# Moving the weight tiles 96 bytes apart, and the probabilities by 32, in a kernel of attention and two feed-forward layers

## The chip, the cores and the metric

The kernel runs on one core of one Trainium2 chip. The metric is the device time of one launch in microseconds (us); lower is better. PE is TensorE, DVE is VectorE, ACT is ScalarE, POOL is GpSimd, SP is SyncE. SBUF is the on-chip memory; an address here is a byte offset inside a partition, the same in all 128 partitions.

## The reference

Three layers follow each other. `q`, `k` and `v` have 2 batches of 8 heads, 768 positions and width 64; `x` between the layers has 1536 tokens of width 512; the two hidden widths are 2048 and 1536.

```python
mask = q_bucket[:, :, :, None] == k_bucket[:, :, None, :]   # buckets: signs of q @ proj, k @ proj
scores = np.where(mask, scale * q @ k.T, -1e9)
attn = np.exp(scores - max); attn /= attn.sum(-1) + 1e-9
x = (attn @ v)                      # heads side by side: 1536 x 512
h = x @ w_in;  x = (h * np.cos(h)) @ w_out
g = x @ w_gate
out = (g * sigmoid(g) * (x @ w_val)) @ w_out2
```

All data are float32.

## The kernel before

The order of the work is written out by hand (the pools run in manual schedule), so each engine gets its instructions in the order in which the code issues them.

**Attention** (about 15 to 232 us of the trace). Two heads run as a pair. The scores of a block of 128 queries are four matmuls of 384 columns (lines 540 and 543), in a float32 form called float32r, with operands split into a high and a low part. DVE writes the block of probabilities `p` out of PSUM (L550), ACT applies the exponential in place (L561), POOL scales it in place (L579), PE transposes it in six pieces of 128 columns, plain float32 (L600, `t<-ident,p`: the identity `ident` is the moving operand, `p` the stationary one), and ACT or DVE copies the result. The product with `v` is L618.

**The first feed-forward layer** (about 232 to 483 us). For each of 48 pairs of token block and hidden block, `hidden` makes `h` and `out1` adds its product with `w_out`. The weights lie in tiles of two parts, high and low, of 128 x 512 each: ACT writes the high part, POOL the low one (`split_hi`). Each product is three matmuls, high by high, high by low, low by high (`each_of_three`, its matmul has line 804). In `h` and `out1` the weight tile is the stationary operand, 128 of its columns at a time, and the activations (`xh`, `xl`, `g..h`, `g..l`) move, 512 columns each. Twelve matmuls make one `h`, twelve the four pieces of one `out1`.

**The second feed-forward layer** (about 483 to 764 us). A form with seven products in place of eight makes `gate` and `val`: here too the weights (`prepare`, three tiles with tag `sp` and one with tag `sp4`) are stationary and activations of 384 columns move, six matmuls a product. Between them stand matmuls of `out2`, mostly in runs of six, where the activation `uh` or `ul` is stationary and the weight tile (tag `spo`, `prepare_out`) moves, 512 columns.

**Addresses.** A weight tile has 2 x 512 x 4 = 4096 bytes in each partition. The pool `late` holds three plain tiles `w`, six buffers `sp` from byte 130016 on, two buffers `raw`, and four buffers `spo` from 162784 on. In the built program every operand of every float32r matmul starts at a multiple of 512 bytes plus 480; the eight buffers of `p` start at a multiple of 512 plus 32 and `ident` at one plus 128.

Of the kernel before, what the change touches and what calls it, by code (L numbers as in the profile page):

```python
# [10 lines left out]
F32 = mybir.dt.float32  # L11
F32R = mybir.dt.float32r
# [5 lines left out]
P = 128  # L18
# [9 lines left out]
def lsh_attention_moe_moe2(  # L28
# [15 lines left out]
    NB = proj.shape[1]  # L44
    NT, DM = out.shape
# [18 lines left out]
    NL, NR = 3, 10  # L64
    NPP = NC2 // 2
    NSPO = 4

    ctx.enter_context(tc.manual_schedule())

# [32 lines left out]
    }  # L102
    done = {"fetch": 0}
    pools = {}

    def fetch_next():
        i = done["fetch"]
        if i == len(items):
            return
        done["fetch"] += 1  # L110
        nm, c = items[i]
        pool = pools["late"] if i >= NATT and i % 2 else early
        raw = pool.tile([P, DM, 2], I32, tag="raw", bufs=2, name=f"raw{i}")
        w = sources[nm].bitcast(I32)
        if nm in ("out", "out2"):
            nc.sync.dma_start(
                out=raw.rearrange("p f t -> p (f t)"), in_=w[c * P : (c + 1) * P, :]
            )
        else:
            nc.sync.dma_start(  # L120
                out=raw.rearrange("p (a f) t -> p a (f t)", a=NCC),
                in_=w.rearrange("(a p) f -> p a f", p=P)[:, :, 2 * c * P : 2 * (c + 1) * P],
            )
        raws[i] = raw
# [73 lines left out]
            fetched[nm, n] = t  # L198

    def split_hi(nm, n, pool=None, tag="sp", bufs=6):  # L200
        t = (pool or pools["late"]).tile([P, 2, DM], F32R, tag=tag, bufs=bufs, name=f"{nm}{n}s")
        w = fetched.pop((nm, n), None)
        if w is None:
            w = stored[nm, n % NC1]
        nc.scalar.activation(out=t[:, 0, :], in_=w, func=AF.Copy)
        parts[nm, n] = t
        return lambda: nc.gpsimd.tensor_tensor(
            out=t[:, 1, :], in0=w, in1=t[:, 0, :].bitcast(F32), op=ALU.subtract
        )

    def split(nm, n, **place):
        if (nm, n) not in parts:
            split_hi(nm, n, **place)()
# [10 lines left out]
    pre = actx.enter_context(tc.tile_pool(name="pre", bufs=1))  # L224
# [1 line left out]
    sm = actx.enter_context(tc.tile_pool(name="sm", bufs=4))  # L226

    pj0 = {nm: pre.tile([P, D], F32, tag="pj0" + nm, name="pj0" + nm) for nm in "qk"}
    pjs = pre.tile([P, NB], F32, tag="pjs", name="pjs")
    crow = pre.tile([1, 2, P], F32, tag="crow", name="crow")  # L230
    one = pre.tile([1, 1], F32, tag="one", name="one")

# [635 lines left out]
    for u in range(NU):  # L868
        pr, i = divmod(u, NBLK)
# [158 lines left out]
    def two_parts(t, src):  # L1028

        nc.scalar.activation(out=t[:, 0], in_=src, func=AF.Copy)  # L1030
        return lambda: nc.gpsimd.tensor_tensor(
            out=t[:, 1], in0=src, in1=t[:, 0].bitcast(F32), op=ALU.subtract
        )

    def prepare(nm, m):


        if m >= NSTEP:
            return
        p0, p1 = fetched.pop((nm, m, 0)), fetched.pop((nm, m, 1))  # L1040
        A11, A12, A21, A22 = p0[:, : 2 * P], p0[:, 2 * P :], p1[:, : 2 * P], p1[:, 2 * P :]
        x, y = (
            pools["right"].tile([P, 2, 2 * P], F32, tag="w", bufs=NR, name=f"{nm}{m}{a}")
            for a in "xy"
        )
        t = [
            pools["late"].tile([P, 2, 2, 2 * P], F32R, tag="sp", bufs=6, name=f"{nm}{m}t{i}")
            for i in range(3)
        ]
        t4 = pools["right"].tile([P, 2, 2 * P], F32R, tag="sp4", bufs=2, name=f"{nm}{m}t3")  # L1050

        pieces[nm, m] = {
            1: t[0][:, :, 0], 2: t[0][:, :, 1], 6: t[1][:, :, 0], 7: t[1][:, :, 1],
            5: t[2][:, :, 0], 3: t[2][:, :, 1], 4: t4,
        }
        lo = two_parts(t[0].rearrange("p t a f -> p t (a f)"), p0)
        nc.vector.tensor_tensor(out=y[:, 0], in0=A21, in1=A22, op=ALU.add)
        yield
        lo()
        (nc.gpsimd if (nm, m) == ("gate", 1) else nc.vector).tensor_tensor(out=x[:, 0], in0=y[:, 0], in1=A11, op=ALU.subtract)  # L1060
        yield
        nc.vector.tensor_tensor(out=x[:, 1], in0=A11, in1=A21, op=ALU.subtract)
        yield
        nc.vector.tensor_tensor(out=y[:, 1], in0=A12, in1=x[:, 0], op=ALU.subtract)
        lo = two_parts(t[1], x)
        yield
        lo()
        lo = two_parts(t[2], y)
        yield
        lo()  # L1070
        lo = two_parts(t4, A22)
        yield
        lo()

    def prepare_out(m, k):
        t = pools["late"].tile([P, 2, DM], F32R, tag="spo", bufs=NSPO, name=f"out2_{m}_{k}s")
        two_parts(t, fetched.pop(("out2", m, k)))()
        parts["out2", m, k] = t

# [114 lines left out]
    def out2(m, order=("11", "22", "21", "12")):  # L1194
# [9 lines left out]
        for i, q in enumerate(order):  # L1204
# [4 lines left out]
            for c in range(HB):  # L1209
                s, ts_ = half * HB + c, slice(c * P, (c + 1) * P)  # L1210
                ends = m == NSTEP - 1 and s == NBLK - 1
                if ends and seen:
                    for (pool, tag), cs in zip(banks, (slice(0, 2 * P), slice(2 * P, DM))):
# [4 lines left out]
                        o = pools["late"].tile(  # L1218
                            [P, 2 * P], F32, tag="spo", bufs=NSPO, name=f"ol{cs.start}"
                        )  # L1220
# [8 lines left out]
                if ends:  # L1229
                    part = pools["late"].tile([P, DM], F32, tag="spo", bufs=NSPO, name="olp")  # L1230
                    nc.scalar.activation(out=part, in_=acc[s], func=AF.Copy)
# [22 lines left out]
    for n in range(2, N1):  # L1254
# [10 lines left out]
        if n >= 3:  # L1265
# [3 lines left out]
        g = times(n - 1)  # L1269
        lows = [  # L1270
            split_hi(*use, **({"tag": "spo", "bufs": NSPO} if n + 2 >= N1 else {}))
            for use in uses[n + 2]
        ]
# [17 lines left out]
        if n == 2 * NC1 + 2:  # L1291
            tsum = token_sums(
                0,
                lambda i, name: pools["late"].tile(
                    [P, 2, HALF], F32, tag="spo", bufs=NSPO, name=name
                ),
            )
        next(tsum, None)
        if n == N1 - 5:
            fetch_group("gate", 0)  # L1300
            first = prepare("gate", 0)
# [10 lines left out]
    for m in range(NSTEP):  # L1312
# [12 lines left out]
        for nm in ("gate", "val"):  # L1325
            nxt = ("val", m) if nm == "gate" else ("gate", m + 1)
            after = ("gate", m + 1) if nm == "gate" else ("val", m + 1)
            ready = prepare(*nxt)

            def chores(k):  # L1330
                if k == 0:
                    fetch_group(*after)
                next(ready, None)
                rows = {("val", 0, 0): [0], ("val", 0, 2): [1], ("val", 0, 3): [2], ("val", 0, 5): [3]}
                out1_close(N1 - 1, rows.get((nm, m, k), []))
                if nm == "gate" and k == 3:
                    fetch2("out2", m, 0)
                    fetch2("out2", m, 1)
                if nm == "val" and k in (1, 3):
                    prepare_out(m, 0 if k == 1 else 1)  # L1340
                if 1 <= m < 5 and k in (2, 5):
                    next(tsum, None)
                if m == NPP - 1 and nm == "val" and k in (2, 4, 5, 6):
                    next(tsum, None)

            if m == 0:
                counts = (2, 2, 2, 2, 2, 3, 3) if nm == "gate" else (2, 2, 2, 2, 0, 2, 2)
            elif m == 1 and nm == "gate":
                counts = (6, 0, 4, 0, 4, 0, 0)
            else:  # L1350
                counts = (6, 0, 6, 0, 6, 0, 0) if nm == "gate" else (0, 6, 0, 6, 0, 6, 0)
            group(nm, m, filler, counts, chores)
            for _ in ready:
                pass
# [36 lines left out]
```

## Time and profile before

| | us |
|---|---|
| median of 3 runs | 769.82 (769.77 to 770.27) |
| the profiled execution | 770.41 |
| its span, first to last instruction | 768.5 |
| PE busy | 761.5 |
| DVE busy | 547.9 |
| ACT busy | 520.8 |
| POOL busy | 487.2 |

The span is what the trace shows; 1.9 us of the execution lie around it. Matmuls overlap in the pipeline, so the busy time of one matmul (0.39 us) is longer than the time from its start to the next one's start. That distance, called pitch below, is what PE's work costs. It is read from the chain of work that ended last, whose pieces give the start, the length and the number of matmuls in a row.

### The profile page before, as it was taken

The page shows a single profiled execution, that of the slowest core. Times are in us where ns is not written, and L with a number is a line of the kernel's source. Part 1 is how long each engine was busy: PE and PEld are TensorE (multiplying, and loading weights), DVE is VectorE, ACT ScalarE, POOL GpSimd, SP SyncE. Part 2 cuts the span into 40 slices and gives each one's busy share as a digit, 9 for nine tenths or more (in the row PEclk, how much of TensorE's full clock was granted, in tenths as well). Part 3 has the DMA queues.
Part 4 walks back from the last instruction along what each step waited for, and adds up shares of the span by engine and source line. Part 5 has one row for each costly group of instructions (what it writes and reads, how often), then busy time and mean ns, then how long its engine had stood idle before and what let it go on. Part 6 is the DMA issues. An engine that isn't in the chain of part 4 may idle for free.

```text
span 768.5 us, 12675 instructions
## 1 busy us (share of the span) xinstructions
PE 761.5 (99%) x4107; PEld 640.1 (83%) x4107; DVE 547.9 (71%) x1092; ACT 520.8 (68%) x1020; POOL 487.2 (63%) x424
## 2 busy tenths in 40 slices
PE   8999999999999999999999999999999999999998
PEld 5777868777777888888888888999999999999996
DVE  7777778777755787766666798587776787665553
ACT  7778887988878788887788777653444454444433
POOL 5647555554556776777778988666665595656450
PEclk9999999999999999999999999999999999999999
DMA  7577576757115777688866755122222215221102
GB/s 217 135 180 165 164 191 150 202 164 179 56 55 174 243 261 255 205 309 285 280 186 217 239 175 185 42 70 82 70 54 72 69 27 205 70 82 43 42 1 83
DMA packets 72692, 113.01 MB, mean 147 GB/s; under 512 B 6675, under 2 KB 44979, under 8 KB 72627
## 3 DMA queue, kind: packets, MB, share of 16 engines
q1 hardware_dynamic: 72352, 112.08, 48.7%
q8 instruction: 33, 0.54, 0.3%
q14 instruction: 33, 0.26, 0.1%
q10 hardware_dynamic: 274, 0.13, 0.1%
HBM read 76.29 MB, written 18.35 MB: 123 GB/s over the span
## 4 chain that ended last, share of the span: by engine, by line
PE 97%; ACT 1%; DVE 1%; issue 0%; POOL 0%; DVEq 0%
PE o L804 30%; PE h L804 17%; PE av L618 8%; PE t L600 8%; PE s L540 4%; PE s L543 4%; PE pj L341 1%; PE trk L285 1%; PE trq L285 1%; ACT p L561 1%; PE gate6Y L804 0%; PE gate7Y L804 0%; PE gate0Y L804 0%; PE val6Y L804 0%; PE val5Y L804 0%; PE val2Y L804 0%
## 5 line engine op out<-in xcount | busy, mean ns | idle before, releaser
L579 POOL TENSOR_SCALAR p<-p,rv 128x768 f32<-128x768 f32 x96 | 89.0, 944 | 68.3 <-DVE rv L572 61.6
L550 DVE TENSOR_SCALAR_CACHE_REDUCE p<-s 128x768 f32<-128x768 f32 x96 | 91.5, 955 | 26.7 <-PE s L543 10.6
L561 ACT ACTIVATE p<-p,mn 128x768 f32<-128x768 f32 x96 | 89.0, 934 | 2.9 <-DVE p L550 2.7
L606 ACT ACTIVATE pt<-t 128x384 f32<-128x384 f32 x140 | 63.9, 488 | 23.8 <-PE t L600 23.6
L600 PE MATMUL t<-ident,p 128*128 128x128 f32 x576 | 79.1, 274 | 0.6 <-POOL p L579 0.5
L600 PEld LDWEIGHTS t<-ident,p 128*128 128x128 f32 x576 | 66.8, 140 | 13.6 <-POOL p L579 6.2
L618 PE MATMUL av<-pt,vn 128*64 128x384 f32 x384 | 66.0, 491 | 0.0
L1108 ACT ACTIVATE uh<-u 128x384 fp32r<-128x384 f32 x48 | 23.8, 521 | 59.1 <-DVE u L1103 59.1
L835 DVE SCALAR_TENSOR_TENSOR rf<-ki,h 128x512 f32<-128x512 int32 x47 | 32.7, 696 | 39.3 <-ACT ki L832 39.3
L540 PE MATMUL s<-Y,X 128*128 128x384 f32 x192 | 57.6, 381 | 0.5 <-DVE p L550 0.3
L618 PEld LDWEIGHTS av<-pt,vn 128*64 128x64 f32 x384 | 26.2, 137 | 34.9 <-issue 34.7
L847 ACT ACTIVATE r<-r 128x512 f32<-128x512 f32 x48 | 30.3, 632 | 31.1 <-DVE r L839 30.9
L859 DVE TENSOR_TENSOR g<-h,r 128x512 f32<-128x512 f32 x48 | 33.0, 687 | 24.6 <-ACT r L848 24.0
L543 PE MATMUL s<-W,Z 76*128 76x384 f32 x192 | 49.4, 339 | 0.7 <-DVE Z L469 0.5
L1097 ACT ACTIVATE sg<-gate 128x384 f32<-128x384 f32 x36 | 18.9, 525 | 43.0 <-DVE gate L1148 42.9
L139 ACT ACTIVATE w<-raw 128x512 f32<-128x512 f32 x68 | 44.9, 662 | 2.0 <-DMA raw<-in_moe_w_in_dram 2.0
L804 PE MATMUL o<-out_1s,uh 128*128 128x512 f32 x144 | 45.0, 392 | 0.0
L804 PE MATMUL o<-out_0s,uh 128*128 128x512 f32 x142 | 44.3, 392 | 0.0
L155 DVE TENSOR_SCALAR bw<-w 128x512 int32<-128x512 int32 x55 | 37.8, 688 | 3.2 <-ACT w L139 2.0
L832 ACT ACTIVATE ki<-h 128x512 int32<-128x512 f32 x48 | 28.3, 590 | 14.9 <-PE h L804 14.8
L160 DVE SCALAR_TENSOR_TENSOR w<-raw,bw 128x512 int32<-128x512 int32 x55 | 37.3, 679 | 0.3
L848 ACT ACTIVATE r<-r,halfpi 128x512 f32<-128x512 f32 x48 | 34.8, 725 | 1.5
(1824 smaller groups left out, 2389.4 us busy)
## 6 DMA issues: line engine op xcount, KB each, us to landing
f<-w SPq DMA_DIRECT2D x58, 256.0 KB
raw<-in_moe_w_out_dram SPq DMA_DIRECT2D x28, 512.0 KB
raw<-in_moe_w_in_dram SPq DMA_DIRECT2D x16, 512.0 KB
raw<-in_moe_w_gate_dram SPq DMA_DIRECT2D x12, 512.0 KB
raw<-in_moe_w_val_dram SPq DMA_DIRECT2D x12, 512.0 KB
Y<-kH SPq DMA_DIRECT2D x28, 192.0 KB
vn<-in_v_dram SPq DMA_DIRECT2D x8, 384.0 KB
gate_0f<-f SPq DMA_DIRECT2D x12, 256.0 KB
```

Of the source, the lines that this page charges most:

```text
L139: nc.scalar.activation(out=t, in_=raws[i][:, :, 1].bitcast(F32), func=AF.Prelu, scale=2.0**-112, alpha=-(2.0**32),)
L155: nc.vector.tensor_scalar(out=word, in0=ti, scalar1=3, scalar2=None, op0=ALU.logical_shift_left)
L160: nc.vector.scalar_tensor_tensor(out=ti, in0=low, scalar=29, in1=word, op0=ALU.logical_shift_right, op1=ALU.bitwise_or)
L540: nc.tensor.matmul(out=ps[:, e, :HALF], lhsT=X[:, j, qs], rhs=Y[:, j, ks], start=True, stop=False)
L543: nc.tensor.matmul(out=ps[:, e, :HALF], lhsT=Z[:KZ, j, qs], rhs=W[:KZ, j, ks], start=False, stop=True)
L550: nc.vector.tensor_scalar(out=pt.rearrange("p (e s) -> p e s", e=2), in0=ps[:, :, :HALF], scalar1=-MASKED, scalar2=None, op0=ALU.min, op1= ...
L561: nc.scalar.activation(out=pt, in_=pt, func=AF.Exp, bias=nbias.pop((u, j)), scale=-1.0, accum_out=sums[u][:, j : j + 1],)
L579: nc.gpsimd.tensor_scalar(out=pt, in0=pt, scalar1=rv[:, j : j + 1], scalar2=1.0, op0=ALU.mult, op1=ALU.mult)
L600: nc.tensor.transpose(ps[:, c * P : (c + 1) * P], src[:, kb * P : (kb + 1) * P], ident)
L606: nc.scalar.activation(out=o, in_=s3, func=AF.Copy)
L618: nc.tensor.matmul(out=ps[j * D : (j + 1) * D, :HALF], lhsT=nat["v", pr][:, j, BLOCKS[kb], :], rhs=pts[half, j][:, kb, :], start=(kb == 0) ...
L804: nc.tensor.matmul(out=out_ap, lhsT=s, rhs=m, start=first and i == 0, stop=last and i == 2, **flags)
```

## The change

A helper `padded` allocates a tile 24 elements (96 bytes) longer and returns the part without the padding. The tiles of `split_hi`, the three `sp` tiles of `prepare` and the tiles of `prepare_out` come from it. So the six `sp` buffers move by 0, 96, 192, 288, 384 and 480 bytes, the two `raw` buffers of `late` by 576, the four `spo` buffers by 576, 672, 768 and 864. The first four weight tiles, which stand in another pool, and the `sp4` tiles stay where they were. A small tile of the pool `pre` becomes 32 bytes longer, which moves what lies behind it by 32: the transposed `q` and `k`, and the eight buffers of `p`.

No instruction is added, removed or reordered; operands have other addresses. Because the `late` tiles now cover slightly different bytes of earlier tiles, one wait on a POOL instruction (the low part of the second weight tile) moves on ACT, from the conversion of `w16` (L139) to that of `w15`.

```diff
+    PAD = 24
...
+    def padded(pool, shape, dtype, pad=PAD, **place):
+
+        n = math.prod(shape)
+        t = pool.tile([P, n + pad], dtype, **place)[:, :n]
+        if len(shape) == 2:
+            return t.rearrange("p (a b) -> p a b", b=shape[1])
+        return t.rearrange("p (a b c) -> p a b c", b=shape[1], c=shape[2])
...
     def split_hi(nm, n, pool=None, tag="sp", bufs=6):
-        t = (pool or pools["late"]).tile([P, 2, DM], F32R, tag=tag, bufs=bufs, name=f"{nm}{n}s")
+        t = padded(pool or pools["late"], [2, DM], F32R, tag=tag, bufs=bufs, name=f"{nm}{n}s")
...
-    pjs = pre.tile([P, NB], F32, tag="pjs", name="pjs")
+    pjs = pre.tile([P, 8 + NB], F32, tag="pjs", name="pjs")[:, :NB]
...
         t = [
-            pools["late"].tile([P, 2, 2, 2 * P], F32R, tag="sp", bufs=6, name=f"{nm}{m}t{i}")
+            padded(pools["late"], [2, 2, 2 * P], F32R, tag="sp", bufs=6, name=f"{nm}{m}t{i}")
             for i in range(3)
         ]
...
     def prepare_out(m, k):
-        t = pools["late"].tile([P, 2, DM], F32R, tag="spo", bufs=NSPO, name=f"out2_{m}_{k}s")
+        t = padded(pools["late"], [2, DM], F32R, tag="spo", bufs=NSPO, name=f"out2_{m}_{k}s")
```

## Rows read from the trace of the kernel before

**Rows 1.** The page: busy time by engine; PE's share and granted clock in 40 slices.
```profile
PE 761.5 (99%) x4107; PEld 640.1 (83%) x4107; DVE 547.9 (71%) x1092; ACT 520.8 (68%) x1020; POOL 487.2 (63%) x424
...
PE   8999999999999999999999999999999999999998
...
PEclk9999999999999999999999999999999999999999
```

**Rows 2.** Waits of PE in the span: who waited for whom, us, times, longest.
```profile
PE cv L667 <- DVE one L658: 1.4, 1, 1.4
PE t L600 <- POOL p L579: 0.5, 1, 0.5
PE s L543 <- DVE Z L469: 0.5, 1, 0.5
PE s L540 <- DVE p L550: 0.3, 1, 0.3
PE s L543 <- ACT W L466: 0.2, 1, 0.2
```

**Rows 3.** PE by stretch: length, busy us, instructions, granted clock, DMA share, GB/s.
```profile
30.00:222.00 192.00, 191.96 (x1339) 1.00 0.60 152
222.00:480.00 258.00, 258.00 (x1149) 1.00 0.69 228
480.00:756.00 276.00, 275.93 (x1439) 1.00 0.21 65
```

**Rows 4.** Chain that ended last, first feed-forward layer: start us, length us, what.
```profile
238.11 2.72 PE h L804 x12
240.83 2.72 PE o L804 x12
243.55 2.72 PE h L804 x12
```

**Rows 5.** The same chain, second feed-forward layer.
```profile
615.95 1.39 PE o L804 x6
617.34 1.04 PE val5Z L804 x6
618.38 1.04 PE gate6X L804 x6
619.42 1.39 PE o L804 x6
...
483.98 0.47 PE o L804 x2
484.44 1.05 PE gate0Y L804 x6
```

**Rows 6.** The same chain, attention: two transposes, then the two score lines.
```profile
171.19 0.66 PE t L600 x6
171.84 0.33 PE trk L285 x3
172.17 0.35 PE s L540 x2
```

**Rows 7.** Weight loads by line: count, busy us, mean ns of one, idle before.
```profile
L600 PEld LDWEIGHTS t<-ident,p 128*128 128x128 f32 x576 | 66.8, 140 | 13.6 <-POOL p L579 6.2 <-issue 4.3 <-POOL kT L366 0.2
L540 PEld LDWEIGHTS s<-Y,X 128*128 128x128 f32 x192 | 29.2, 191 | 3.4 <-DVE p L550 1.4 <-POOL Y L439 0.8 <-DVE rv L572 0.6
L804 PEld LDWEIGHTS o<-out_1s,uh 128*128 128x128 f32 x144 | 26.6, 188 | 3.6
```

**Rows 8.** PE in order of time where a new run of matmuls begins.
```profile
232.34 0.50 PE L804 MATMUL h<-xh,in2s 128*128 128x512 f32 x1
232.68 0.40 PE L804 MATMUL h<-xl,in2s 128*128 128x512 f32 x1
232.92 0.63 PE L804 MATMUL h<-xh,in2s 128*128 128x512 f32 x2
...
235.00 0.39 PE L804 MATMUL h<-xh,in2s 128*128 128x512 f32 x1
235.23 0.39 PE L804 MATMUL o<-g0h,out0s 128*128 128x512 f32 x1
235.46 0.39 PE L804 MATMUL o<-g0l,out0s 128*128 128x512 f32 x1
```

**Rows 9.** The chain around 500 us, where it leaves PE.
```profile
498.65 1.16 DVE gate1x L1062
499.81 0.60 DVE xl L956
```

## The prediction

> **What bounds the kernel now.** I read the page first: PE is busy 99% of the span and no other engine over 71%, at a granted clock of 0.9 or more in every slice [rows 1]. Then the waits of PE: five, 2.9 us in all [rows 2]; asked for 30 to 768 us alone, the same view has no row. By stretch PE is busy in 191.96 of 192, 258.00 of 258 and 275.93 of 276 us, at a granted clock of 1.00, so at the upper level, 2.4 GHz [rows 3]. PE is therefore never kept waiting by another engine that the profile can name. The span is a sum of pitches, and an edit that changes no instruction can only act through the pitch, or make another engine so slow that PE begins to wait.
>
> So the pitch has to be taken apart. In the first layer twelve matmuls of 512 columns take 2.72 us, 226.7 ns each, whatever line they belong to [rows 4]. In the second layer six matmuls of 384 columns take 1.04 us, 173.3 ns each [rows 5]. The difference, 53.3 ns for 128 columns, is 0.417 ns a column, one column per cycle at 2.4 GHz. The columns then make 213.3 and 160.0 ns, and **13.3 ns** are left over per matmul in both lengths: 32 cycles. Plain float32 transposes come to 0.33 us for three, 110 ns for 128 columns [rows 6]; taken as two passes of 53.3 ns they leave only 3.3 ns over. Each of these matmuls loads new weights while the one before it streams. Beside a stream at half rate that load is nearly free; beside one at full rate it leaves 13.3 ns, and the load itself is recorded at 188 to 191 ns in place of 140 [rows 7].
>
> The 13.3 ns are not a constant. Where a run starts after other work, the pitches are 0.24 and 0.23 us and reach 0.227 only some ten matmuls later, with the same tiles and the same order [rows 8]. The runs of six in `out2` never get that far: 1.39 us for six, 231.7 ns each, 5.0 ns over the settled 226.7 [rows 5]. So the price depends on how the two streams of PE, the moving columns and the next weights, stand to each other in time. Other engines don't show in it: DMA goes from 0.21 to 0.69 of its share between stretches [rows 3], and the settled pitch does not move.
>
> **The change part by part.**
>
> *Addresses of the weight tiles.* Before, moving and stationary operands of every float32r matmul stand at the same place in 512 bytes. Counted in the built program, 2,067 of the 2,979 float32r matmuls have another distance after: 360 of `h`, 552 of `out1`, 720 of `gate` and `val`, 435 of `out2`. If what the two streams disturb is shared by address, a shift in bytes acts like a shift in time, and the trace bounds the effect from both sides. At best the load becomes as cheap as beside the transposes: 13.3 - 3.3 = 10.0 ns each, 2,067 x 10.0 = 20.7 us, and the 5.0 ns of the roughly 396 `out2` matmuls in runs go too, 2.0 us: -22.7 us. At worst a moved pair is as unsettled as `out2` is now: +5.0 ns. That is 912 x 5.0 = 4.6 us for `h` and `out1`; the 720 of `gate` and `val` go from 1.04 us for six to the 1.05 that rows show near 484 us [rows 5], at most 10 ns in six with rounding, so I double it to 3 ns each, 2.2 us: +6.8 us; `out2` is there already. No row has a pair at another distance, so neither end is near. The tiles stand at five different distances, some of which may help and some harm, so I take the **middle per matmul** of -10.0 and +5.0 ns, -2.5 ns: 2,067 x -2.5 = **-5.2 us**.
>
> *The probabilities.* The 576 transposes load `p` beside `ident`, at 110 ns with 3.3 ns to lose or win: 0 to -1.9 us if all of it went; if they were to cost the 13.3 ns, +5.8 us. Their stream runs at half rate, where the present distance of 96 bytes costs next to nothing, and I take 0. DVE, ACT and POOL read and write `p` in place at the new address. Nothing in the trace says that this costs more; if it did, it would lie beside PE's 192 us of uninterrupted work [rows 3], and what would come late first is the transposes behind POOL's scaling, where the weight loads already stood idle for 6.2 us [rows 7].
>
> *The moved wait and the `raw` tiles.* The wait goes from one conversion on ACT to the one before it and asks for the low part of the layer's second weight tile, which POOL writes before PE's `h` runs shown in [rows 4]. Queued behind it on ACT are `cosine` and the high parts; they are covered by PE's unbroken stretch of 258 us. I take 0, and some 0.5 us, like the longest waits behind POOL or DVE after the start [rows 2], if the cover failed. Destinations of DMAs move by 576 bytes; no queue is passed and nothing is late: 0. The one place where the chain leaves PE is DVE's at 498.65 us, 1.16 and 0.60 us [rows 9]; its operands do not become slower unless SBUF addresses slow DVE.
>
> *Sum.* The profiled execution took 770.41 us, 768.5 of it span. 770.41 - 5.2 = 765.2. It lies 0.6 us above the median of the runs, so **764.6 us** on the scale of the runs.
>
> **A rule against it.** The row shows 13.3 ns left over at 1.00 of the clock, the same for 384 and 512 columns [rows 4, 5]. The Trainium skill, "TensorE: Matmul & The Clock Gate", section "Weight-path perf modes", gives a fast weight load of 128 weights in 128/4 = 32 cycles, on where the type is not FP32; 32 cycles at 2.4 GHz are an estimate of 13.3 ns, by that page, and would be there at any address. The Trainium skill, "SBUF — State Buffer", section "Who interferes with whom", gives PE two independent read ports. By these the sum would be 0 and the time 769.8. The trace agrees with the 32 cycles of the settled pitch and not with the spread before it settles.
>
> **Rivals.**
>
> *Nothing happens (769.8 us).* The leftover is a fixed price of changing weights at full rate and the settling has to do with clocks alone. For it: the settled 13.3 ns is the same for two lengths and for tiles all over SBUF; other engines never disturb it. Against it: the settling itself. The change then also fails to do what its bytes suggest: every term is 0.
>
> *It gets slower (776 us).* The present equal distance is what lets runs settle at 226.7. With a different distance for each tile, every `h` and every `out1` begins unsettled, twelve matmuls are about as long as settling takes [rows 8], and the runs stay near 231.7. Price: the upper bound above, +6.8 us on the 769.8; it decides for slower once about a quarter of the moved pairs, some 300 of `h` and `out1`, stay unsettled and none gain. For it: `out2`, whose runs of six don't settle. Against it: the `gate` and `val` runs between, also six long, are at 173.3 ns and settled.
>
> *The whole price goes (747 us).* Two streams at different distances don't meet at all; -22.7 us. For it: the transposes, whose operands stand 96 bytes apart and leave 3.3 ns. Against it: they stream at half rate, which explains that alone.
>
> **How the numbers follow.** A measurement of this kernel can tell about 0.2%, 1.5 us, from no change. Forecast, a partial gain of 1.5 to 17 us around 764.6: 0.40. Nothing, within 1.5 us: 0.36. Slower: 0.18. The whole price or nearly: 0.06. Faster is 0.46, same 0.36, slower 0.18. Cases of both signs hold most of the chance; the forecast's own range is 753 to 768. For eight in ten I go down to 753, where nearly the whole-price case is left out (0.06), and up to 773.5, half-way through the slower rival, leaving out 0.12.
>
> **What would show it.** Right: the chain's pieces of twelve shorter than 2.72 us in `h` or `out1` for some tiles and not for others, and `out2` runs under 1.39. Rival one: 2.72, 1.04 and 1.39 again. Rival two: pieces of twelve near 2.78. Whole price: near 2.60 and 0.98. In all of them the transposes stay at 0.66 for six and PE shows no waits after 30 us. Wrong altogether would be a new wait of PE on DVE, ACT or POOL, or transposes with another pitch.

## The result, and the profile after

The changed kernel takes **776.73 us** (776.05 to 777.91, 6 runs) against 770.25 us (769.77 to 770.59, 6 runs) for the kernel before on the same chip: a ratio of 1.0086, 95% interval 1.0073 to 1.0099. It is slower by 0.9%. The forecast was 764.6 us with a range up to 773.5, so both the sign and the range were wrong. The rival that ends slower, priced at 776, had a chance of 0.18. Among all executions behind this document two were disturbed, one of the kernel before (1275.8 us) and one of the kernel with the padding alone (3285.71 us); they stand in no figure here.

The profiled execution took 776.86 us, with a span of 774.8: 6.3 us more span than before. The page, its first group (engine, busy time, instructions):

```profile
span 774.8 us, 12675 instructions
...
PE 767.5 (99%) x4107; PEld 640.3 (83%) x4107; DVE 552.6 (71%) x1092; ACT 522.4 (67%) x1020; POOL 485.2 (63%) x424
```

PE has 6.0 us more, and still fills the span; the number of instructions is the same as in [rows 1]. The waits of PE are the five of [rows 2], 3.1 us in all in place of 2.9, all of them before 30 us, and by stretch (length, PE busy, count, granted clock, DMA share) PE is as full as in [rows 3]:

```profile
222.00:483.00 261.00, 261.00 (x1139) 1.00 0.69 225
483.00:762.00 279.00, 278.93 (x1448) 1.00 0.20 64
```

So nothing waits that did not wait before. The matmuls themselves are further apart: 1,139 in 261 us, where [rows 3] have 1,149 in 258. The chain of work that ended last, in the first feed-forward layer (start us, length us, what), has lost the one length of [rows 4], 2.72 us for twelve:

```profile
243.63 2.79 PE h L813 x12
246.42 2.79 PE o L813 x12
249.21 2.75 PE h L813 x12
251.96 2.81 PE o L813 x12
254.77 2.74 PE h L813 x12
257.51 2.80 PE o L813 x12
...
488.26 0.87 PE gate0X L813 x5
```

The beginnings of the two layers in the kernel before, same view:

```profile
232.41 2.99 PE h L804 x12
...
482.91 1.06 PE gate0X L804 x6
```

The six lengths of the changed kernel come back in this order for the whole layer, as the six `sp` buffers come round. Their tiles stand at six distances; by *distance* is meant the address of the moving operand less that of the weights, modulo 512. In the order of the rows they are 128, 224, 320, 416, 0 and 32. Together the six pieces make 16.68 us where 6 x 2.72 = 16.32 were before. The second layer begins at 488.26 us in place of 482.91, the first one at 232.40 in place of 232.41: **5.35 us are lost in the first layer**, the remaining 0.95 in the second. To see where, take from both traces the distance from each matmul's start to the next start, and compare them matmul by matmul: `h` is 1.88 us longer in all, `out1` 3.53, `gate` and `val` 0.59, `out2` 0.42; the other work is about 0.1 us shorter. In the second layer (same view, the changed kernel) the `out2` runs are at 1.38 to 1.41 us for six, against 1.39 in [rows 5]; `gate` and `val` runs are mostly at 1.04 to 1.06, against mostly 1.04:

```profile
618.23 1.41 PE o L813 x6
619.64 1.05 PE val5Z L813 x6
620.68 1.04 PE val5Y L813 x6
621.73 1.38 PE o L813 x6
```

In the same view, ahead of the layers, the transposes have their 0.66 us for six and 0.33 for three [rows 6]:

```profile
171.15 0.66 PE t L609 x6
171.81 0.33 PE trk L294 x3
```

### The profile page after: what moved, and what is told of

Same layout as the page of the kernel before. It is cut to its first block, busy times and chain, and to the rows that moved or that the text cites. A ratio compares the mean times of both kernels' runs of the same rounds, so it can differ in the third digit from the quotient of the medians.

```text
span 774.8 us, 12675 instructions
## 1 busy us (share of the span) xinstructions
PE 767.5 (99%) x4107; PEld 640.3 (83%) x4107; DVE 552.6 (71%) x1092; ACT 522.4 (67%) x1020; POOL 485.2 (63%) x424
## 4 chain that ended last, share of the span: by engine, by line
PE 97%; ACT 1%; DVE 1%; issue 0%; POOL 0%; DVEq 0%
PE o L813 30%; PE h L813 17%; PE av L627 8%; PE t L609 8%; PE s L549 4%; PE s L552 4%; PE pj L350 1%; PE trk L294 1%; PE trq L294 1%; ACT p L570 1%; PE gate6Y L813 0%; PE gate7Y L813 0%; PE gate11Y L813 0%; PE gate3Y L813 0%; PE gate10Y L813 0%; PE gate2Y L813 0%
## 5 line engine op out<-in xcount | busy, mean ns | idle before, releaser
L552 PEld LDWEIGHTS s<-W,Z 76*128 76x128 f32 x192 | 34.7, 189 | 1.5 <-ACT W L475 1.5
```

What stands on the lines that cost most here:

```text
L552: nc.tensor.matmul(out=ps[:, e, :HALF], lhsT=Z[:KZ, j, qs], rhs=W[:KZ, j, ks], start=False, stop=True)
```

## Experiments

Two theories of the loss were put against each other. **D**: each distance between the two operands has its own pitch. **M**: it is the change of distance from tile to tile that keeps runs from settling, which is what the slower rival of the prediction said.

### Which half of the change

The first kernel has only the longer small tile, the second only the padding.

```diff
-    pjs = pre.tile([P, NB], F32, tag="pjs", name="pjs")
+    pjs = pre.tile([P, 8 + NB], F32, tag="pjs", name="pjs")[:, :NB]
```

> Only the small tile of `pre` is longer, so only `p` and the transposed `q` and `k` move by 32 bytes. Theory A (the price comes from the weight tiles): 770, as before; transposes 0.66 us for six, twelve of `h` and `out1` in 2.72. Rival (the probabilities carry part of it): 772 or more, with a longer attention part before 232 us.

> Only the weight tiles lie 96 bytes further apart. Theory A: the whole loss, 776 to 777, `h` near 2.75 and `out1` near 2.80 for twelve. Rival: less than 775, the rest belonging to the probabilities.

The first measured 770.30 us, ratio 0.9999 (0.9990 to 1.0009), the second 776.79 us, ratio 1.0083 (1.0065 to 1.0101). The probabilities cost nothing and the padding is the whole loss. In the chain of the first kernel, ahead of the layers, the transposes are as before:

```profile
171.12 0.66 PE t L600 x6
171.77 0.33 PE trk L285 x3
...
251.65 2.72 PE o L804 x12
254.37 2.72 PE h L804 x12
```

### One distance for all tiles

A gap ahead of the `sp` buffers moves `sp`, `raw` and `spo` together; 24 elements are 96 bytes, 128 are 512.

```diff
+    pools["late"].tile([P, 24], F32, tag="gap", bufs=1, name="gap")
     for m in (2, 3):
         for use in uses[m]:
             split(*use)
```

> All `sp`, `raw` and `spo` buffers move by the same 96 bytes (a gap ahead of them), so each weight tile stands at the same distance from its partner, and that distance is not zero in 512. Theory D (each distance has its own price): the pitch that the changed kernel shows at this distance, near 234 ns for `h` and `out1`, is had by all of them: 1,152 x 7 ns = 8 us, 778. Theory M (a distance that changes from tile to tile is what unsettles the runs): 2.72 us for twelve again, 770.

> The same gap, 512 bytes. The distances modulo 512 are those of before. Theory D with a period of 512 or a divisor of it: 770 and 2.72 us for twelve. Rival (what matters has a longer period, or it is the mere place of the pool): slower, up to 778. Theory M: 770.

Moved by 96 bytes: 779.75 us, ratio 1.0125 (1.0109 to 1.0141). Moved by 512: 770.12 us, ratio 0.9999 (0.9989 to 1.0008). The chain of the first:

```profile
242.95 2.81 PE h L804 x12
245.76 2.81 PE o L804 x12
248.58 2.81 PE h L804 x12
251.39 2.81 PE o L804 x12
```

and of the second:

```profile
254.04 2.72 PE h L804 x12
256.76 2.72 PE o L804 x12
```

Theory M falls: in the first layer there is one distance for all moved tiles, so nothing changes from tile to tile, and this kernel is slower than the changed one. 2.81 us are 234.2 ns a matmul, in `h` and `out1` alike. That is what the changed kernel has in its one `out1` of three at distance 416, which is the distance here. (In `out2`, where the weight tile is the moving operand, the same shift makes the distance 96.) Theory D holds, and its period divides 512. These two kernels issue the same instructions in the same order as the kernel before, with the wait on ACT where it was; so the loss does not need the moved wait.

### The distance, or the place

> All late weight tiles move by 32 bytes, their partners stay. Theory D: one new distance, 480 in 512, with a price of its own that no run has shown alone: somewhere between the 226.7 of before and 234, so 770 to 779, and the same for every `h` and `out1`. If the price were set by 64-byte pieces of the stationary operand, whose start is now a multiple of 64, `h` and `out1` would gain up to 6.7 ns: 762.

> A gap ahead of everything on the left side of SBUF moves the activations, their high and low parts, `p`, `ident` and the weight tiles by 32 bytes together; the pool on the right, with some moving operands of `gate` and `val` and the `sp4` tiles, stays. Theory D (only the distance between the two operands counts): `h` and `out1` 2.72 us for twelve as before, `out2` 1.39 for six, 770 within 1. Rival (the place of an operand in a line of SBUF counts): the same `h` and `out1` as in the run that moves the weight tiles alone by 32 bytes.

The first has the gap ahead of the `sp` buffers again, with 8 elements. The second has its gap ahead of the first tile of the kernel, so that moving and stationary operands of `h`, `out1` and `out2` shift together:

```diff
+    cpool.tile([P, 8], F32, tag="gap", name="gap")
     ident = cpool.tile([P, P], F32, tag="ident", name="ident")
```

The weight tiles moved alone: 778.24 us, ratio 1.0105 (1.0088 to 1.0122). With everything on the left: 771.29 us, ratio 1.0015 (1.0006 to 1.0024). The chain of the first of them, then of the second:

```profile
252.37 2.80 PE o L804 x12
255.17 2.80 PE h L804 x12
```

```profile
251.91 2.72 PE o L805 x12
254.63 2.72 PE h L805 x12
...
614.50 1.05 PE val5Z L805 x6
615.55 1.06 PE val5Y L805 x6
616.61 1.36 PE o L805 x6
```

The same weight tiles stand at the same addresses in both. With partners that moved along, the pitch is the old one; without, it is 233.3 ns. So in the first layer the distance counts and not the place of an operand in a line. The gain of 6.7 ns for starts at a multiple of 64 did not come either. What the second kernel loses (0.15%) lies only in part where expected. Compared matmul by matmul with the kernel before, the 432 of `gate` and `val` whose distance changed, because their moving operand stands on the right and did not shift, cost 0.33 us; the 576 whose distance is still 0 cost 1.34 us, and `out2`, also still at 0, gains 0.72 us. Of the rows shown, `val5Z` is at the new distance, `val5Y` and `out2` are at 0. In these short runs what stands before a run shows in its length; that the place plays no part there is not shown. The expectation of 770 within 1 missed that by 0.3 us, and that `out2` falls to between 1.36 and 1.39 was not expected at all.

### A survey in steps of 64

This edit is made in the changed kernel, with the small tile of `pre` as it was before:

```diff
-    PAD = 24
+    PAD = 16
```

> Weight tiles 64 bytes further apart in place of 96, nothing else: `sp` move by 0 to 320 in steps of 64, `spo` by 384 to 576. A survey of distances. Theory D: a pitch for each distance, the one at 192 bytes as in the changed kernel (229 ns in `h`), buffers at 0 and at 512 as before; in all 772 to 778. If distances that are multiples of 64 were harmless: 770.

775.70 us, ratio 1.0071 (1.0056 to 1.0086). The chain (distances 0, 192, 256, 320, 384, 448, in the order of the rows):

```profile
238.17 2.72 PE h L813 x12
240.89 2.80 PE o L813 x12
243.69 2.75 PE h L813 x12
246.43 2.75 PE o L813 x12
249.19 2.79 PE h L813 x12
251.98 2.80 PE o L813 x12
254.78 2.75 PE h L813 x12
```

Multiples of 64 are not harmless. The last row stands at distance 0 again and takes 2.75, since its first seven matmuls are at 224 to 236 ns and only from the eighth on at 227: what the run before left is still seen in them. The first row, with a run at distance 0 before it, takes 2.72. Distance 256 looked like 0 here, which the next two runs took up.

> All late weight tiles move by 256 bytes. In the run with tiles 64 bytes apart, an `h` at this distance began at 231 to 236 ns and was at 226.7 from its seventh matmul on. Theory D (a distance has a settled pitch of its own, whatever stands around it): uniform 256 settles at 226.7 as uniform 0 does, `h` and `out1` 2.72 for twelve, 770. Theory M (any distance but zero costs, and the seven were a return to the old state): above 2.75, 775.

> All late weight tiles move by 192 bytes. Between other distances, twelve matmuls at this one went round 229.2, 231.6, 225.9 ns, 228.9 on average, and those of `gate` and `val` had 173.6 ns. Theory D: the same round throughout, 2.75 for twelve: 1,100 x 2.2 = 2.5 us more, about 0.8 us less in `gate` and `val`, 772. Rival: with one distance everywhere it settles at 226.7: 769 to 770.

Both have the gap ahead of the `sp` buffers, with 64 and with 48 elements. By 256 bytes: 770.43 us, ratio 1.0002 (0.9993 to 1.0011). By 192: 773.31 us, ratio 1.0038 (1.0023 to 1.0053). The chain of the first, and of the second:

```profile
251.75 2.72 PE o L804 x12
254.47 2.72 PE h L804 x12
```

```profile
251.88 2.75 PE o L804 x12
254.63 2.75 PE h L804 x12
```

256 cannot be told from 0, in time or in the pieces: the period is 256 bytes, or a divisor of it, and of the divisors the steps of 32 leave none, since 32, 64 and 128 are all dearer than 0. Other pairs agree: `h` has 2.79 at 128 (the changed kernel) and at 384, `out1` 2.80 at 192 and at 448. The expected 772 for 192 bytes counted on 0.8 us less in `gate` and `val`, which came out unchanged (+0.03 us), while `out2`, at distance 192, cost 0.43 us; `h` and `out1` did as foretold.

### Only the moving weight tiles of `out2`

In `out2` the `spo` tiles are the moving operand. A gap behind the `raw` buffers, of 88, 80 or 64 elements, moves the `spo` buffers alone. They also hold the last two weight tiles of `out1`, 24 matmuls.

```diff
+        if n == 2 * NC1:
+            pools["late"].tile([P, 88], F32, tag="gap", bufs=1, name="gap")
```

> Only the `spo` tiles move, all by 352 bytes, the distance at which the changed kernel's `out2` had 228.5 ns in place of 232.2. Theory D: about 429 x 3.7 ns = 1.6 us less, 768.6; the first feed-forward layer unchanged. Rival (the mix of distances around it made that pitch): 770 or more.

> Only the `spo` tiles move, by 320 bytes; they are the moving operand of `out2`, so the distance is plus 320, the one that went round at 228.9 ns where the weights were the stationary operand. If distances of one value act alike whichever operand has moved: 400 x 3.3 = 1.3 us less, 769. If the sign of the distance or the entry into each run of six decides: 770 to 772, as with 352 bytes.

> Only the `spo` tiles move, by 256 bytes, the other distance that settles at 226.7, after about six matmuls. Runs of `out2` are six long, so settling helps little: 231 ns a matmul in place of 231.7, 770 within 0.5. A gain of 1 us or more would say that runs enter this distance nearer to its settled state.

By 352: 771.08 us, ratio 1.0012 (1.0003 to 1.0022). By 320: 771.20 us, ratio 1.0012 (1.0002 to 1.0021). By 256: 770.28 us, ratio 1.0000 (0.9990 to 1.0009). The chains of the first and of the second:

```profile
636.16 1.40 PE o L804 x6
637.56 1.04 PE val6Z L804 x6
638.60 1.04 PE val6Y L804 x6
```

```profile
634.12 1.06 PE val6X L804 x6
635.17 1.05 PE val6Y L804 x6
636.22 1.38 PE o L804 x6
```

None is faster. The 228.5 ns of the first expectation was a misreading: it is the mean over the changed kernel's `out2` matmuls at distance 352 with five of 256 columns among them, at 117 to 125 ns each; without these the mean is 233.6 ns. The runs of six at this distance take 1.40 us in the changed kernel too, 233 ns each, and a run of the shorter matmuls stands at its end (chain of the changed kernel):

```profile
632.40 1.40 PE o L813 x6
...
638.09 1.40 PE o L813 x6
...
770.42 0.38 PE o2l L813 x3
```

So this distance has one pitch in both kernels, as theory D says, and it is dearer than distance 0: matmul by matmul, `out2` costs 0.81 us more than in the kernel before and `gate` and `val` 0.10 us less. At 320 the `out2` runs do get shorter, 0.54 us in all, and the `gate` and `val` runs behind them longer, 1.05 and 1.06 in place of 1.04 us and 1.21 us in all, though their own distance is unchanged; the sum is a loss.

### The last distance

> All late weight tiles move by 160 bytes. The runs so far give seven of the eight distances that steps of 32 bytes make in a period of 256; this is the last, 352 in 512, and the only one that could still lie under the 226.7 ns of distance 0. Theory D with every distance but 0 dearer: 229 to 234 ns, 2.75 to 2.81 for twelve, 773 to 780. Rival (0 is only one cheap distance among others): 226.7 or less, 770 or under.

The gap ahead of the `sp` buffers has 40 elements. 780.07 us, ratio 1.0125 (1.0108 to 1.0142). The chain:

```profile
252.19 2.80 PE o L804 x12
254.99 2.80 PE h L804 x12
```

All eight distances that 32-byte steps make in 256 now have a length for twelve matmuls of 512 columns:

| distance modulo 256 | us for twelve | ns each | from |
|---|---|---|---|
| 0 | 2.72 | 226.7 | the kernel before; moved by 256 and by 512 |
| 32 | 2.80 | 233.3 | the changed kernel, between others |
| 64 | 2.75 | 229.2 | moved by 192 |
| 96 | 2.80 | 233.3 | moved by 160 |
| 128 | 2.79 | 232.5 | the changed kernel, between others |
| 160 | 2.81 | 234.2 | moved by 96 |
| 192 | 2.80 | 233.3 | 64 bytes apart, between others |
| 224 | 2.80 | 233.3 | moved by 32 |

The kernel before stood at the cheapest. No version beats it by more than the noise: the fastest, moved by 512 bytes, has a ratio of 0.9999.

## Why the prediction was wrong

**That only the pitch can act** was right. No wait was added after 30 us, and the 6.3 us that the span grew are longer distances between matmuls.

**That a shift in bytes acts like a shift in time** was put as a condition. What the runs show is less: the pitch depends on the distance in bytes. Whether it does so through time is not shown.

**The probabilities, the moved wait and the `raw` tiles at 0** were right; the kernel with the longer small tile alone shows it for the first. The moved wait has no run of its own, but the kernels with one shift for all tiles keep the wait in its old place, and three of them are slower than the changed kernel.

**The middle of the bounds is the step that failed.** The term was 2,067 matmuls at -2.5 ns, -5.2 us. Measured, the first layer costs +5.35 us, 5.9 ns for each of its 912 moved matmuls, and the second layer +0.95 us. The lower bound, -10.0 ns, rested on the 3.3 ns that the transposes leave over. The text itself said that these stream at half rate, and still used them as an end for streams at full rate; no distance came below the 13.3 ns of distance 0. And distance 0 was treated as one point among many with the average somewhere near. The rows gave no such average: the only pitches away from the settled 226.7 that the trace of before has, 0.24 and 0.23 us in [rows 8] and the 231.7 of [rows 5], are all dearer. Going by these nearest rows would have given the upper end. Nor is the term the middle of the prediction's own bounds: -22.7 and +6.8 us have theirs at -8.0, and the term is smaller because it takes +5.0 ns for every matmul, where the upper bound has 3 ns for `gate` and `val` and nothing for `out2`. The moved matmuls stand at nine distances, not five, since the `spo` buffers add 64, 160, 256 and 352; the 120 at 256 are as good as unmoved.

**The upper bound** was nearly the answer, +6.8 us against 6.45, though not term by term, so that its closeness is in part luck: `h` and `out1` 4.6 against 5.35 us, `gate` and `val` 2.2 against 0.59, `out2` 0 against 0.42.

**The slower rival** had the price, 776, its sign, pieces of twelve near 2.78 (2.74 to 2.81 were seen), and its first sentence: the equal distance is what lets runs settle at 226.7. Its second, that it takes a different distance for each tile, was wrong; one distance for all is worse when it is 96 or 160 modulo 256, and runs at those distances keep a dearer pitch from the first matmul to the last. Its threshold was off as well: 300 of the 2,067 moved pairs are a seventh, not a quarter. The unsettled beginnings it pointed to exist, as the last row of the survey in steps of 64 shows, 2.75 for 2.72, but they are the smaller part.

**The rule against the change** described the floor only. What is left over at 2.4 GHz is 13.3 ns at distance 0, 32 cycles, and 234.2 - 213.3 = 20.9 ns at distance 160, 50 cycles; so it is not the same at any address. The Trainium skill, "TensorE: Matmul & The Clock Gate", section "Weight-path perf modes", gives the 32 cycles as the theory of a fast weight load for fp8, with no win for fp32. The trace has that count at distance 0 and at none of the other seven, and no run shows that it is this load. The Trainium skill, "SBUF — State Buffer", section "Who interferes with whom", lists PE's two read ports as independent and says that PE never waits on anyone. In these runs the pitch depends all the same on where the two operands stand, by 7.5 ns a matmul between distances 0 and 160.

**Open.** Why the distance sets the pitch, and why with a period of 256 bytes, no run shows; nor why 13.3 ns stay at distance 0. Nor is it shown which pair counts: a matmul's own two operands, or its moving operand and the weights that are loaded for the next matmul beside it. Within a run of twelve both pairs have the same distance modulo 512. Distances that are not a multiple of 32 bytes were not tried. The lengths at 32, 128 and 192 were read between runs at other distances, and may lie somewhat off their settled values.

## What to carry to other kernels

Where PE is full and no wait is left, look at the pitch, per line and per tile: two lengths for the same matmul are a cost that no list of waits names. In a stream of float32r matmuls like these, whose weights change each time, keep the moving operand and the weights at the same place modulo 256 bytes, and be wary of padding tiles for its own sake. And where a term has never been seen, do not take the middle between an end borrowed from another kind of work and one that the rows show; the rows nearest in kind were all on one side.

## What the runs showed of the hardware that was not expected

The pitch of float32r matmuls with new weights each time depends on where their two operands stand to each other in SBUF, with a period of 256 bytes: 2.72 us for twelve at distance 0, 256 and 512, 2.81 us at 416. These kernels issue the same instructions in the same order, PE waits for nothing after 30 us in any of them, and the granted clock is 1.00 in all. Why it is so stays open. Plain float32 transposes, with the identity as moving operand, have the same 0.66 us for six at distances 96 and 64.
